# Second tile's attention in two separate parts, its moves on GpSimd's queue and its normalization on VectorE; weight loads spread over the first tile

## The chip, the cores and the metric

The kernel runs on one core of a Trainium2 chip. The core has five engines that run their own instruction streams side by side: TensorE (PE in the profile; PEld is its weight load) for matrix products, VectorE (DVE), ScalarE (ACT) and GpSimd (POOL) for elementwise work, and SyncE (SP), which here only issues DMA transfers. Other engines can issue DMAs too; each issues in the order of its own stream. The metric is the device time of one execution in microseconds (us).

## What is computed

Two stages follow each other: attention within chunks of 64 positions, and a feed-forward block with a bounded quadratic activation.

```python
scores = scale * np.matmul(q_c, k_c.transpose(0, 1, 2, 4, 3))
scores = scores - np.max(scores, axis=-1, keepdims=True)
attn = np.exp(scores)
attn = attn / (np.sum(attn, axis=-1, keepdims=True) + 1e-09)
out = np.matmul(attn, v_c)
...
h = x @ w_in
g = np.where(pos, h, np.where(neg, 0.0, (h + beta) ** 2 / (4.0 * beta)))
return (g @ w_out).astype(np.float32)
```

Here q, k and v have 8 batches, 8 heads, 576 positions of 64 numbers; x is the attention's output as 4608 tokens of 512 numbers; w_in is 512 x 2048 and w_out 2048 x 512, both given as 64-bit floats.

## The kernel before

**Tiles.** The 4608 tokens are cut into nine tiles of 512 (`t` from 0). For each tile the attention runs in four head pairs (`g` from 0 to 3), and the feed-forward in sixteen steps (`j` from 0 to 15), one for each 128 columns of w_in.

**Attention of a head pair.** `attn_turn` brings q and k into transposed form (qT, kT): for the first tile through TensorE (`flip`) and a copy by ScalarE, for later tiles by VectorE's block transposes (L372). `scores_of` and `values_of` give the two groups of 64x64 products. Between them, `attn_softmax` takes the maximum (L450), subtracts it, exponentiates and sums; the second tile instead gives the scaled negative maximum (L455) to ScalarE's exponential, which also sums (L459). Then come a small addition and a reciprocal (L476, L477), the normalization (L482: GpSimd for the first two tiles, VectorE for the others), and the transposition: for later tiles a block transpose by VectorE into the one buffer x (L504) and eight DMAs that put the blocks of x in their places in aT (`move`, L494, on SyncE's queue). Values read aT and v. `attn_split` cuts the values into a high part xh (ScalarE, L517) and a residue xl (VectorE, L518), the operands of the feed-forward. All scores and values from the second tile on share one pair of accumulation banks, ps_a.

**Feed-forward.** Products are made of three parts (high by high, high by low, low by high). `ffn_in` has twelve products for a step (L533, into ps_h), followed by ScalarE's relu and square and VectorE's bounds (r, L544); `ffn_split` makes gh and gl of r (L553, L554); `ffn_out` has twelve products for a step (L568, into four banks ps_o), two steps behind `ffn_in` (LAG). I call twelve such products a block.

**Weights.** The 32 weight pieces (wi0 to wi15, wo0 to wo15, 0.5 MB each) are loaded as 64-bit words in the first tile's time (`load_weight`) and turned into high and low 32-bit parts by `prepare`: three operations of ScalarE (L259, L265, L284) and four of VectorE (L262, L269, L274, L288). The parts take the place of the words and stay for all nine tiles. The first tile's attention borrows the places of the last weights.

**What sets the order.** The kernel's code only lists parts of work with `plan.add`: engine, an assumed cost, what is read and written. `Plan.emit` then runs a model of the engines: whenever an engine is free, it takes the part that was listed first among those that the model holds to be ready, and the instructions are emitted in this order. Each engine's stream is therefore fixed beforehand, and on the chip an instruction that has to wait holds up all that stands behind it on its engine. Where TensorE would be idle at the start, the planner puts in products without use (`warm`, L688 and L691) that keep the clock up; they end with the first use of bank ps_h1.

**Around the change.** The main loop lists, at each feed-forward step j of tile t, work of the attention of tile t+1: at j = 0, 4, 8, 12 the transposes of a head pair, at j = 2, 6, 10, 14 one part of work that has the values of a head pair and the scores of the next (`attention`, one `attn_products` call for both), with its split, its softmax and the next loads. Weight loads are listed early: twelve among the loads of the second tile's first head pairs, and up to three at each step (`load_more(3)`); they wait for nothing but their place. Two weights are prepared at each step.

## Time and profile before

| what | value |
|---|---|
| time, median of 3 runs (lowest to highest) | 885.51 us (885.17 to 887.1) |
| the profiled execution, its own time | 884.54 us |
| span of the profiled execution (first to last instruction) | 882.8 us |
| mean granted TensorE clock | 0.992 |
| ScalarE busy | 379.6 us |
| DMA, mean over the span | 72 GB/s |
| DMA, first four slices of 22 us | 213, 290, 251, 267 GB/s |

The span is 1.74 us shorter than the execution's own time. In the profile a line such as L533 is the line of the listing above. "busy" is the time in which an engine executes instructions; a row of a timeline gives start, length, engine, line, operation and tiles (written <- read), and in brackets how long the engine sat idle before it and what ended that. Lengths of neighbouring rows overlap by some hundredths of a microsecond, so a price is better taken from start to start. SPq and POOLq rows are DMA issues of these engines.

### The profile page before, as it was taken

The numbers are of one execution on the slowest core, as the hardware profiler recorded it, in microseconds if no ns is written. First come the engines' busy times: TensorE is split into PE (matmuls) and PEld (weight loads), VectorE is DVE, ScalarE is ACT, GpSimd is POOL, SyncE is SP. The second block draws the span as 40 slices with busy tenths as digits, with TensorE's granted clock in tenths as the row PEclk, the third lists the DMA queues.
The fourth block names the chain that finished last, engine by engine and source line by source line (L and its number), as shares of the span: only waits on it lengthen the run. The fifth ranks groups of instructions, "written<-read, shape, count | busy, mean of one in ns | idle before, by whom it ended". The sixth has DMA issues, their size and how long they took to land.

```text
span 882.8 us, 15026 instructions
## 1 busy us (share of the span) xinstructions
PE 863.6 (98%) x5924; PEld 707.5 (80%) x5924; DVE 451.2 (51%) x771; ACT 379.6 (43%) x691; POOL 20.2 (2%) x30
## 2 busy tenths in 40 slices
PE   9799996999999999999999999999999999999998
PEld 8688775888888888888888888888888888888886
DVE  4999994444454445444544454444444444423222
ACT  4898873333333333333433333334333333333332
POOL 6000000000000000000000000000000000000000
PEclk9999997999999999999999999999999999999999
DMA  9988335322242224222322233223222321001001
GB/s 213 290 251 267 67 67 122 54 48 49 49 96 49 48 45 100 48 49 47 92 49 47 47 72 63 47 42 79 53 48 43 66 54 25 13 1 49 0 1 48
DMA packets 265158, 63.92 MB, mean 72 GB/s; under 512 B 249984, under 2 KB 258176, under 8 KB 265088
## 3 DMA queue, kind: packets, MB, share of 16 engines
q1 hardware_dynamic: 263520, 61.65, 31.8%
q0 software_dynamic: 512, 1.05, 0.5%
q8 instruction: 47, 0.77, 0.4%
q10 hardware_dynamic: 1056, 0.26, 0.2%
q14 instruction: 23, 0.19, 0.1%
HBM read 45.09 MB, written 9.44 MB: 62 GB/s over the span
## 4 chain that ended last, share of the span: by engine, by line
PE 89%; DVE 7%; SPq 1%; issue 1%; ACT 1%; DMA 1%; POOL 0%; DVEq 0%; POOLq 0%; ACTq 0%
PE ps_h L533 42%; PE ps_o L568 41%; PE ps_a L417 2%; PE ps_a L396 2%; PE ps_h L688 1%; DVE tmp L269 1%; DVE tmp L274 1%; SPq L319 1%; DVE r L544 1%; DVE tmp L262 1%; DVE parts_wi L288 1%; SPq L494 0%; DMA q_sb<-in_q_dram 0%; DVE parts_wo L288 0%; DVE mx L450 0%
## 5 line engine op out<-in xcount | busy, mean ns | idle before, releaser
L533 PE MATMUL ps_h<-xh,parts_wi 128*128 128x512 f32 x1152 | 387.2, 396 | 4.6 <-DVE r L544 2.9
L568 PE MATMUL ps_o<-parts_wo,gh 128*128 128x512 f32 x1152 | 355.6, 390 | 1.0 <-DVE parts_wo L288 1.0
L533 PEld LDWEIGHTS ps_h<-xh,parts_wi 128*128 128x128 f32 x1152 | 218.0, 189 | 53.2 <-DVE r L544 4.0
L568 PEld LDWEIGHTS ps_o<-parts_wo,gh 128*128 128x128 f32 x1152 | 216.0, 188 | 47.0 <-DVE parts_wo L288 1.6
L544 DVE SCALAR_TENSOR_TENSOR r<-ps_h,r 128x512 f32<-128x512 f32 x144 | 98.0, 681 | 261.0 <-ACT r L543 261.0
L533 PE MATMUL ps_h<-xl,parts_wi 128*128 128x512 f32 x576 | 226.6, 393 | 1.7 <-DVE xl L518 1.7
L568 PE MATMUL ps_o<-parts_wo,gl 128*128 128x512 f32 x576 | 224.2, 389 | 0.7 <-DVE gl L554 0.7
L540 ACT ACTIVATE r<-ps_h 128x512 f32<-128x512 f32 x144 | 86.1, 598 | 284.4 <-PE ps_h L533 284.4
L553 ACT CAST gh<-r 128x512 fp32r<-128x512 f32 x144 | 89.5, 622 | 148.9 <-PE ps_o L568 114.7
L554 DVE TENSOR_TENSOR gl<-r,gh 128x512 fp32r<-128x512 f32 x144 | 98.4, 683 | 107.2 <-ACT gh L553 106.9
L533 PEld LDWEIGHTS ps_h<-xl,parts_wi 128*128 128x128 f32 x576 | 109.1, 189 | 24.7 <-DVE xl L518 3.1
L568 PEld LDWEIGHTS ps_o<-parts_wo,gl 128*128 128x128 f32 x576 | 108.1, 188 | 23.5 <-DVE gl L554 1.0
L543 ACT ACTIVATE r<-r 128x512 f32<-128x512 f32 x144 | 91.0, 632 | 3.5
L450 DVE TENSOR_REDUCE mx<-ps_a 128x8 f32<-128x512 f32 x34 | 23.4, 689 | 20.5 <-ACT xh L517 18.8
L417 PEld LDWEIGHTS ps_a<-aT,v_sb 64*64 64x64 f32 x1056 | 18.6, 134 | 15.1 <-issue 13.4
L517 ACT CAST xh<-ps_a 128x512 fp32r<-128x512 f32 x34 | 19.9, 585 | 22.0 <-PE ps_a L396 21.1
L417 PE MATMUL ps_a<-aT,v_sb 64*64 64x64 f32 x1056 | 23.2, 224 | 3.6 <-DMA aT<-x 3.6
L475 DVE TENSOR_REDUCE sm<-e 128x8 f32<-128x512 f32 x30 | 20.5, 685 | 10.1 <-ACT e L469 9.9
L504 DVE STREAM_TRANSPOSE x<-e 128x512 f32<-128x512 f32 x32 | 22.7, 710 | 2.2 <-DMA q_sb<-in_q_dram 1.2
L372 DVE STREAM_TRANSPOSE qT<-q_sb 128x512 f32<-128x512 f32 x32 | 22.5, 703 | 0.0
L518 DVE TENSOR_TENSOR xl<-ps_a,xh 128x512 fp32r<-128x512 f32 x34 | 22.3, 657 | 0.2 <-ACT xh L517 0.2
L372 DVE STREAM_TRANSPOSE kT<-k_sb 128x512 f32<-128x512 f32 x32 | 22.1, 691 | 0.0
(77 smaller groups left out, 390.1 us busy)
## 6 DMA issues: line engine op xcount, KB each, us to landing
words_wi<-in_moe_w_in_dram SPq DMA_DIRECT2D x16, 512.0 KB, 7.2
words_wo<-in_moe_w_out_dram SPq DMA_DIRECT2D x16, 512.0 KB, 7.4
v_sb<-in_v_dram SPq DMA_DIRECT2D x128, 64.0 KB, 2.4
aT<-x SPq DMA_DIRECT2D x256, 32.0 KB, 1.9
out_dram<-tmp SPq DMA_DIRECT2D x32, 256.0 KB, 2.0
q_sb<-in_q_dram SPq DMA_DIRECT2D x112, 64.0 KB, 2.3
k_sb<-in_k_dram SPq DMA_DIRECT2D x112, 64.0 KB, 2.3
q_sb<-in_q_dram SPq DMA_DIRECT2D x32, 32.0 KB, 2.1
```

The source lines that it names most:

```text
L372: plan.add("dve", 0.6, lambda src=src, dst=dst: nc.vector.transpose(out=dst, in_=src), (skey,), (dkey,))
L417: nc.tensor.matmul(out=pair[h * C:(h + 1) * C, half, HALF + n * C:HALF + (n + 1) * C], lhsT=v_sb[rows, of:of + C], rhs=aT[rows, at:at + C] ...
L450: plan.add("dve", 0.6, lambda: nc.vector.tensor_reduce(out=mx4, in_=sc, axis=AX.X, op=ALU.max), pkeys, (mkey,))
L504: plan.add("dve", 0.6, lambda: nc.vector.transpose(out=x, in_=e), (ekey,), (xkey,))
L518: plan.add("dve", 0.6, lambda: nc.vector.tensor_tensor(out=of_tokens(xl), in0=ps, in1=of_tokens(xh.bitcast(F32)), op=ALU.subtract), (*pkey ...
L533: nc.tensor.matmul(out=ps, lhsT=weight["wi", j][:, half, kc * P:(kc + 1) * P], rhs=x, start=(kc == 0 and i == 0), stop=(kc == KC - 1 and i ...
L540: plan.add("act", 0.48, lambda: nc.scalar.activation(out=r, in_=ps, func=AF.Relu, bias=0.5, scale=0.5), (pkey,), (rkey,))
L543: plan.add("act", 0.52, lambda: nc.scalar.square(out=r, in_=r), (), (rkey,))
L544: plan.add("dve", 0.6, lambda: nc.vector.scalar_tensor_tensor(out=r, in0=ps, scalar=1.0, in1=r, op0=ALU.max, op1=ALU.min), (pkey,), (rkey,))
L553: plan.add("act", 0.52, lambda: nc.scalar.copy(out=gh, in_=r), (rkey,), (ghkey,))
L554: plan.add("dve", 0.6, lambda: nc.vector.tensor_tensor(out=gl, in0=r, in1=gh.bitcast(F32), op=ALU.subtract), (rkey, ghkey), (glkey,), port ...
L568: nc.tensor.matmul(out=acc, lhsT=x[:, cols], rhs=weight["wo", j][:, half, :], start=(j == 0 and i == 0), stop=(j == NF - 1 and i == 2),)
```

## The change

Six things change.

- In the first tile's loop the second tile's attention is listed in two kinds of parts: `front` (transposes, scores, softmax) and `back` (values, split), each at a step given by the table `SECOND`. Scores and values of this tile are separate parts on TensorE. The loads of q and k follow each front, those of v each back.
- The eight moves of each head pair of the second tile are issued by GpSimd in place of SyncE.
- The normalization of the second tile runs on VectorE; GpSimd keeps the first tile's.
- Beyond the first ten, a weight load is listed with each preparation and waits for the end of that preparation (`gate`). wi0 and wi1 join the list `order`.
- The planner's assumptions differ: DMA starts at 1.4 in place of 1.68, a weight load moves for 1.4 in place of 1.7, movement is counted for each issuing engine apart, heads loaded by ScalarE or GpSimd take 1.5 times as long.
- The products without use may go on in bank ps_o1 after the first use of ps_h1, in idle time before the first output products.

```diff
-    START, START_DMA = 1.4, 1.68
+    START, START_DMA = 1.4, 1.4
...
             if moving:
-                end = moved = max(end, moved) + moving
+                end = moved[e] = max(end, moved[e]) + moving
...
-        plan.add(queue, 0.65, emit, (), (f"{w}{j}_0", f"{w}{j}_1"), lag=1.7, moving=1.7)
+        plan.add(queue, 0.65, emit, gate["ready"], (f"{w}{j}_0", f"{w}{j}_1"), lag=1.7, moving=1.4)
...
-        plan.add("dve", 0.6, low, (ykey, both[0]), (both[1],), port=True)
+        plan.add("dve", 0.6, low, (ykey, both[0]), (both[1], f"done_{w}{j}"), port=True)
+        gate["ready"] = (f"done_{w}{j}",)
...
-                (), (key,), lag=1.7, moving=rows,
+                (), (key,), lag=1.7, moving=rows if queue == "sp" else 1.5 * rows,
...
-        on_pool = t < 2
+        on_pool = t == 0
...
+        queue = "pool" if t == 1 else "sp"
...
-                    nc.sync.dma_start(
+                    queues[queue].dma_start(
...
-            plan.add("sp", 4.8, move, (xkey,), (akey,), lag=1.7, moving=0.4)
+            plan.add(queue, 4.8, move, (xkey,), (akey,), lag=1.7, moving=0.4)
...
-    load_more(4)
     load_heads(1, 0, "qk")
-    load_more(2)
+    load_next(2)
     load_heads(1, 0, "v")
-    load_more(6)
+    load_next(2)
     load_heads(1, 1)
...
+    def prepare_next():
+        if todo:
+            prepare(*todo.pop(0))
+            load_next()
...
+    def front(t, g):
+        attn_turn(t, g)
+        attn_products(scores_of(t, g))
+        attn_softmax(t, g)
+        if t == 1:
+            load_heads(*divmod(t * NP + g + 2, NP), "qk")
+
+    def back(t, g):
+        attn_products(values_of(t, g))
+        attn_split(t, g)
+        load_heads(*divmod(t * NP + g + 2, NP), "v")
+
+    SECOND = {
+        1: ((front, 0),), 3: ((front, 1),), 5: ((back, 0), (front, 2)), 8: ((back, 1), (front, 3)),
+        11: ((back, 2),), 13: ((back, 3), (front, 4)),
+    }
...
-            attention()
-            load_more(3)
+            if t == 0:
+                for what, g in SECOND.get(j, ()):
+                    what(*divmod(NP + g, NP))
+            else:
+                attention()
             if t < NTILE:
                 ffn_in(t, j)
-            for w, n in todo[:2]:
-                prepare(w, n)
-            del todo[:2]
+            prepare_next()
+            prepare_next()
...
+    def saw(writes, columns):
+        if any(k in ("ps_o0", "ps_o1") for k in writes):
+            if columns != T:
+                return columns == 0
+            fills["turns"] -= 1
+        if "ps_h1" in writes:
+            fills["bank"] = None
+        if fills["bank"] is None and not fills["turns"]:
+            fills["bank"] = o_banks[1][1]
+        return True
```

Because the planner sets the order, the diff doesn't show what stands where. In the rows below a name is the tile's own (wo15, or buffer 0 or 1 of a pair) with a running number behind it, and the changed program's lines lie some lines further down than the old one's.

The first place is TensorE's passage from the first tile to the second. Before, behind the last output products of the first tile (wo15) stood:

```order
L568 MATMUL ps_o23_111<-parts_wo15_1423,gh1_104 128x512 x2
L568 MATMUL ps_o23_111<-parts_wo15_1423,gl1_106 128x512
L417 MATMUL ps_a_112<-aT1_79,v_sb1_73 64x64 x16
L396 MATMUL ps_a_112<-kT0_75,qT0_74 64x64 x16
L533 MATMUL ps_h0_115<-xh3_1_92,parts_wi0_244 128x512
L533 MATMUL ps_h0_115<-xl3_1_100,parts_wi0_244 128x512
L533 MATMUL ps_h0_115<-xh3_1_92,parts_wi0_244 128x512
L533 MATMUL ps_h1_116<-xh3_1_92,parts_wi1_320 128x512
```

that is, the values of the second tile's last head pair (L417), the scores of the third tile's first (L396), and the products of the second tile's steps 0 and 1 that need this pair's xh3 and xl3. Now there stands:

```order
L572 MATMUL ps_o23_111<-parts_wo15_1542,gh1_104 128x512 x2
L572 MATMUL ps_o23_111<-parts_wo15_1542,gl1_106 128x512
L420 MATMUL ps_a_112<-aT0_78,v_sb0_72 64x64 x16
L399 MATMUL ps_a_112<-kT0_75,qT0_74 64x64 x16
L537 MATMUL ps_h0_115<-xh0_1_86,parts_wi2_531 128x512
L537 MATMUL ps_h0_115<-xl0_1_94,parts_wi2_531 128x512
L537 MATMUL ps_h0_115<-xh0_1_86,parts_wi2_531 128x512
L537 MATMUL ps_h0_115<-xh1_1_88,parts_wi2_531 128x512
```

These values and scores are one pair of heads later (aT0 is that of the third tile's first head pair), and only step 2 of the second tile follows: its steps 0 and 1 and the second tile's four values groups now stand ahead of this place, and the feed-forward waits for no attention here.

The second place is VectorE's work around the last two weights, wo14 and wo15. Before:

```order
L269 ISA tmp3_110<-words_wo14_721,tmp3_110 128x1024
L269 ISA tmp0_107<-words_wo15_726,tmp0_107 128x1024
L274 SCALAR_TENSOR_TENSOR tmp3_110<-words_wo14_721,tmp3_110 128x512
L274 SCALAR_TENSOR_TENSOR tmp0_107<-words_wo15_726,tmp0_107 128x512
L554 TENSOR_TENSOR gl0_105<-r0_101,gh0_103 128x512
L288 TENSOR_TENSOR parts_wo14_1417<-tmp3_110,parts_wo14_1417 128x512
L288 TENSOR_TENSOR parts_wo15_1423<-tmp0_107,parts_wo15_1423 128x512
L544 SCALAR_TENSOR_TENSOR r1_102<-ps_h1_116,r1_102 128x512
L450 TENSOR_REDUCE mx1_82<-ps_a_112 128x8
L518 TENSOR_TENSOR xl2_1_98<-ps_a_112,xh2_1_90 128x2x4x64
L455 TENSOR_SCALAR mx1_82<-mx1_82 128x8
L372 STREAM_TRANSPOSE qT0_74<-q_sb0_68 128x512
```

Now, with the sum, the normalization (L485) and the transpose (L508) of the third tile's first head pair shortly ahead of the last weights:

```order
L478 TENSOR_REDUCE sm0_83<-e0_76 128x8
L479 TENSOR_SCALAR sm0_83<-sm0_83 128x8
L480 RECIPROCAL sm0_83<-sm0_83 128x8
L290 TENSOR_TENSOR parts_wo13_1489<-tmp1_108,parts_wo13_1489 128x512
L485 TENSOR_TENSOR e0_76<-e0_76,sm0_83 128x512
L276 SCALAR_TENSOR_TENSOR tmp2_109<-words_wi15_1231,tmp2_109 128x512
L508 STREAM_TRANSPOSE x0_80<-e0_76 128x512
L548 SCALAR_TENSOR_TENSOR r0_101<-ps_h0_115,r0_101 128x512
L290 TENSOR_TENSOR parts_wi15_1505<-tmp2_109,parts_wi15_1505 128x512
```

and then

```order
L558 TENSOR_TENSOR gl0_105<-r0_101,gh0_103 128x512
L290 TENSOR_TENSOR parts_wo14_1536<-tmp3_110,parts_wo14_1536 128x512
L290 TENSOR_TENSOR parts_wo15_1542<-tmp0_107,parts_wo15_1542 128x512
L375 STREAM_TRANSPOSE qT0_74<-q_sb1_69 128x512
L548 SCALAR_TENSOR_TENSOR r1_102<-ps_h1_116,r1_102 128x512
L375 STREAM_TRANSPOSE kT0_75<-k_sb1_71 128x512
```

What moved: the maximum of the second tile's last head pair, the residues of its last two and the whole softmax of the third tile's first one stood behind the last weights, and now stand ahead of them.

The third place is ScalarE's work at the start, around the exponential of the first tile's fourth head pair (it works in the place of wo15). Before:

```order
L284 CAST parts_wo0_460<-tmp3_110 128x512
L265 ACTIVATE words_wi2_233<-words_wi2_233 128x512
L259 ACTIVATE tmp1_108<-words_wo1_240 128x512
L517 CAST xh2_0_89<-ps_a_112 128x512
L469 ACTIVATE first_wo15_118<-first_wo15_118 128x512
L265 ACTIVATE words_wo1_240<-words_wo1_240 128x512
L517 CAST xh1_0_87<-ps_o23_111 128x512
L259 ACTIVATE tmp2_109<-words_wi3_250 128x512
```

Now:

```order
L521 CAST xh0_0_85<-ps_a_112 128x512
L261 ACTIVATE tmp1_108<-words_wo1_265 128x512
L261 ACTIVATE tmp2_109<-words_wi3_271 128x512
L267 ACTIVATE words_wo1_265<-words_wo1_265 128x512
L472 ACTIVATE first_wo15_118<-first_wo15_118 128x512
L267 ACTIVATE words_wi3_271<-words_wi3_271 128x512
L521 CAST xh1_0_87<-ps_o23_111 128x512
```

The scaling of wi3's words (tmp2 <- words_wi3) stood three instructions behind this exponential and now stands two ahead of it. On GpSimd the four multiplications of the second tile are gone, and four groups of eight DMAs from x to aT stand behind those of the first tile.

More of the change, by code (lines that the diff above doesn't have):

```diff
@@ L71, in emit @@
         free["sp"] = self.START_DMA
-        port_free = moved = 0.0
+        port_free = 0.0
+        moved = dict.fromkeys(engines, 0.0)
         soon = {e: [] for e in engines}
@@ L81, in emit @@
                 offer(n)
-        fill_engine, fill_cost, fill_emit, fill_key, fill_columns = filler
+        fill_engine, fill_cost, fill_columns, fill_emit, fill_saw = filler
         filling = True
@@ L100, in emit @@
                 start, e = best
-                if filling and free[fill_engine] < start:
-                    fill_emit()
+                if filling and free[fill_engine] < start and fill_emit():
                     free[fill_engine] = self.products_end(free[fill_engine], fill_cost, fill_columns)
@@ L109, in emit @@
             _, cost, emit, _, lag, columns, port, moving, writes = parts[n]
-            filling = filling and fill_key not in writes
+            filling = filling and fill_saw(writes, columns)
             emit()
@@ L228, in turn_of @@
         return bufs[count[name] % len(bufs)]
+    gate = {"ready": ()}
     def load_weight(w, j, queue="sp"):
@@ L595, in store, with load_next @@
         plan.add("sp", 0.6, send, (okey,), (), lag=1.7, moving=0.8)
+    order = [("wi", 0), ("wi", 1)]
+    for j in range(NF):
+        order.append(("wo", j))
+        if j + 2 < NF:
+            order.append(("wi", j + 2))
+    loads = list(order)
+    def load_next(n=1):
+        for _ in range(n):
+            if loads:
+                load_weight(*loads.pop(0))
     first_loads = [
@@ L606 @@
             load_weight(which, n, queue)
+            loads.remove((which, n))
         else:
             load_heads(0, n, which, queue)
-    order = []
-    for j in range(NF):
-        order.append(("wo", j))
-        if j + 2 < NF:
-            order.append(("wi", j + 2))
     for g in range(NP):
@@ L621 @@
         attn_split(0, g)
-    loads = [o for o in order if (*o, "sp") not in first_loads]
-    def load_more(n):
-        for _ in range(n):
-            if loads:
-                load_weight(*loads.pop(0))
-    load_more(4)
     load_heads(1, 0, "qk")
-    load_more(2)
+    load_next(2)
     load_heads(1, 0, "v")
-    load_more(6)
+    load_next(2)
     load_heads(1, 1)
-    prepare("wi", 0)
-    prepare("wi", 1)
+    def prepare_next():
+        if todo:
+            prepare(*todo.pop(0))
+            load_next()
+    todo = list(order)
+    prepare_next()
[14 more added lines that the diff above has]
+    }
     LAG = 2
-    todo = list(order)
     for t in range(NTILE + 1):
@@ L642 @@
             n = (t + 1) * NP + j // 4
-            if (t, j) == (0, 0):
-                attn_turn(1, 0)
-                attn_products(scores_of(1, 0))
-                attn_softmax(1, 0)
             def attention():
@@ L655, in attention @@
                     if n + 1 < ALL:
-                        attn_products(
-                            values_of(*now), scores_of(*then), lag=0.0 if t == 0 else 0.8
-                        )
+                        attn_products(values_of(*now), scores_of(*then), lag=0.8)
                         attn_split(*now)
@@ L665, in attention @@
                         load_heads(*divmod(n + 2, NP))
-            attention()
-            load_more(3)
+            if t == 0:
[3 more added lines that the diff above has]
+                attention()
             if t < NTILE:
                 ffn_in(t, j)
-            for w, n in todo[:2]:
-                prepare(w, n)
-            del todo[:2]
+            prepare_next()
+            prepare_next()
             m = t * NF + j - LAG
@@ L680 @@
     nc.vector.memset(zeros.bitcast(F32), 0.0)
-    fills = {"n": 0}
+    fills = {"n": 0, "turns": 2 * NP, "bank": h_banks[1][1]}
     def warm():
@@ L685, in warm @@
         fills["n"] += 1
-        ps = h_banks[1][1]
+        ps = fills["bank"]
+        if ps is None:
+            return False
         if n < 28 or n >= 52:
             nc.tensor.matmul(out=ps[:, :P], lhsT=ident, rhs=ident, start=True, stop=True)
-            return
-        cols = (256, 384, T)[(n - 28) // 8]
-        nc.tensor.matmul(
-            out=ps[:, :cols], lhsT=zeros[:, :P], rhs=zeros[:, :cols], start=True, stop=True
-        )
-    plan.emit(("pe", 0.215, warm, "ps_h1", 512))
+        else:
+            cols = (256, 384, T)[(n - 28) // 8]
+            nc.tensor.matmul(
+                out=ps[:, :cols], lhsT=zeros[:, :P], rhs=zeros[:, :cols], start=True, stop=True
+            )
+        return True
[8 more added lines that the diff above has]
+            fills["bank"] = o_banks[1][1]
+        return True
+    plan.emit(("pe", 0.215, 512, warm, saw))
 _INS = ['q', 'k', 'v', 'moe_w_in', 'moe_w_out']
```

## The prediction

> **What bounds the kernel now.** I read the page first, then the windows by stage, then the chain of waits around the end of the first tile, then VectorE's timeline.
>
> ```profile
> span 882.8 us, 15026 instructions
> PE 863.6 (98%) x5924; PEld 707.5 (80%) x5924; DVE 451.2 (51%) x771; ACT 379.6 (43%) x691; POOL 20.2 (2%) x30
> ...
> DVE  4999994444454445444544454444444444423222
> ```
>
> TensorE (PE) is busy for 98% of the span, so only the rest and any time at a lower clock can be won. VectorE (DVE) averages 51%, but its slices say where: 9 from the second to the sixth slice (22 us each), 4 to 5 after.
>
> The windows give each stage's busy time per engine, with instruction counts, and TensorE's granted clock behind them:
>
> ```profile
> 97.00:131.00 34.00, 32.27 (x252) 24.49 (x251) 33.87 (x63) 27.61 (x79) 2.48 (x2) 1.00 0.36 64
> 131.00:149.00 18.00, 11.29 (x100) 8.12 (x98) 8.10 (x16) 5.76 (x15) 1.04 (x1) 0.83 0.59 135
> ...
> 300.00:400.00 100.00, 100.00 (x675) 82.21 (x675) 46.20 (x77) 37.45 (x63) 0.00 (x0) 1.00 0.30 58
> ```
>
> At 97 to 131 us VectorE is full (33.87 of 34.00) and TensorE starts to wait. At 131 to 149 us both idle, and the clock falls to 0.83. From 300 to 400 us TensorE never idles. The loss lies before 154 us. The chain of waits (start, length, what) names it:
>
> ```profile
> 134.62 0.64 SPq L494
> ...
> 139.24 1.93 DMA aT<-x
> ...
> 141.30 0.63 PE ps_a L417 x27
> ...
> 146.36 0.70 DVE sm L475
> 147.08 0.18 DVE sm L476
> ...
> 148.87 4.95 PE ps_h L533 x12
> 153.82 2.74 PE ps_o L568 x12
> 156.56 0.68 PE ps_h L533 x3
> 157.24 0.62 PE ps_a L417 x32
> 157.87 0.47 PE ps_a L396 x32
> 158.33 2.27 PE ps_h L533 x9
> 160.60 2.72 PE ps_o L568 x12
> ```
>
> The last head pair of the second tile is late: SyncE issues its eight moves from 134.62, they land at 141.17, and only then do its values products run (141.30). The next twelve products take 4.95 us where twelve take 2.72 at full clock (160.60). I take as **marker** the start of the second tile's first output block, 153.82; behind it TensorE is full in both programs, so the change is worth what it moves this point. After the marker the old program still does one values-and-scores pair (157.24 to 158.33, 1.09 us; the split block takes 0.68 + 2.27 = 2.95 for 2.72, so 1.32 in all), which the new order does before it. So saving = 153.82 + 1.32 - M, with M the new marker.
>
> **The change part by part.** *The pair's wait goes.* In the new order all four values blocks of the second tile lie inside the first tile's feed-forward. What is late next is VectorE, which must prepare all weights and do the attention before the first tile can end. So M follows from when VectorE has prepared the last two weights, wo14 and wo15. VectorE's timeline of before:
>
> ```profile
> 33.53 1.26 DVE L274 SCALAR_TENSOR_TENSOR tmp<-words_wi,tmp 128x512 uint32<-128x512 uint32 x1
> ...
> 50.38 1.53 DVE L288 TENSOR_TENSOR parts_wi<-tmp,parts_wi 128x512 fp32r<-128x512 f32 x1
> ...
> 99.45 1.58 DVE L262 TENSOR_SCALAR tmp<-tmp 128x512 uint32<-128x512 uint32 x2
> ...
> 114.30 0.75 DVE L262 TENSOR_SCALAR tmp<-tmp 128x512 uint32<-128x512 uint32 x2
> ...
> 115.97 0.69 DVE L288 TENSOR_TENSOR parts_wi<-tmp,parts_wi 128x512 fp32r<-128x512 f32 x1
> 116.58 0.69 DVE L544 SCALAR_TENSOR_TENSOR r<-ps_h,r 128x512 f32<-128x512 f32 x1
> 117.18 0.94 DVE L274 SCALAR_TENSOR_TENSOR tmp<-words_wo,tmp 128x512 uint32<-128x512 uint32 x1
> 118.04 0.70 DVE L504 STREAM_TRANSPOSE x<-e 128x512 f32<-128x512 f32 x1
> 118.67 0.65 DVE L269 CUSTOM_DVE_ANT_0 tmp<-words_wi,tmp 128x1024 uint16<-128x1024 uint16 x1
> ...
> 125.92 1.29 DVE L288 TENSOR_TENSOR parts_wo<-tmp,parts_wo 128x512 fp32r<-128x512 f32 x2
> ```
>
> No idle time stands in these rows. By starts, an operation on 128x512 costs 0.60 (115.97 to 116.58), a transpose 0.62. The last row is wo14 and wo15: wo14 is ready at 126.5. Counted in the two orders, VectorE does these more ahead of that row: two residues xl (1.2), two maxima (1.2), one scaling of a maximum (0.16), one subtraction (0.6), one sum (0.7, row 146.36), two pairs of small operations (0.8, from 0.18 each and the gaps), two x transposes (1.24), two more q and k transposes (1.24), and **five normalizations** (3.0), four of them taken from GpSimd: 10.1 us. Against it, a GpSimd multiplication held VectorE up: 1.53 for 0.69 (50.38), 1.58 for 0.75 (99.45), 0.94 for 0.69 (117.18), 1.9 us in all, which go. So the four normalizations that change engine cost nearly nothing net; what costs is attention that used to come behind the weights. Net +8.2: wo14 at 134.7.
>
> *The start.* VectorE's first 37 operations are the same set; in the old program the next begins at 33.53, of which 0.6 is a GpSimd multiplication's hold (1.26 for 0.69). In the new order ScalarE must scale the words of wi3 before the exponential of the fourth pair:
>
> ```profile
> 22.70 0.43 SPq L237 DMA_DIRECT2D words_wi<-in_moe_w_in_dram  x1
> ...
> words_wi<-in_moe_w_in_dram SPq DMA_DIRECT2D x1, 512.0 KB, 6.9
> ...
> 30.88 0.62 ACT L469 ACTIVATE first_wo<-first_wo 128x512 f32<-128x512 f32 x1
> ```
>
> wi3 lands at 22.70 + 6.9 = 29.6; two ScalarE operations later (about 1.1) the exponential starts at 30.7, as before (30.88). But behind it VectorE now has eight of the 37 left (sum, two small, two xl, a shift, a residue, an addition: 3.8), so it passes this point at about 35.2, 1.65 late, less what of the 0.6 hold falls into this wait. I take 1.5; bounds 0 (same operations) and 2.6 (with a wait for xh in it).
>
> *Small waits* of VectorE for exponentials, now closer behind their maxima: 0 to 2, I take 0.8. wo14 is then ready at 137.0.
>
> *From there to the marker* TensorE does four blocks (2.72 each: out 14, in 1 of the next tile, out 15, in 2) and the pair (1.32): M = 137.0 + 0.1 + 10.9 + 1.3 = 149.3. Saving 155.14 - 149.3 = **5.8 us**. The dive of the clock goes with the wait.
>
> *Moves on GpSimd.* Four times eight issues leave SyncE and go to GpSimd; nothing else stands behind them there after the first tile. The rows are of GpSimd's timeline, then VectorE's beside its issues, then the DMA issues (KB, us to landing):
>
> ```profile
> 1.44 5.03 POOL L338 DMA_DIRECT2D v_sb<-in_v_dram  x8
> ...
> 10.38 1.25 POOL L338 DMA_DIRECT2D first_wo<-in_v_dram  x2 [0.20 <-issue]
> ...
> 50.08 1.29 POOL L482 TENSOR_TENSOR e<-e,sm 128x512 f32<-128x512 f32 x1 [15.83 <-DVE sm L477]
> ```
>
> ```profile
> 11.43 0.68 DVE L269 CUSTOM_DVE_ANT_0 tmp<-words_wi,tmp 128x1024 uint16<-128x1024 uint16 x1
> 12.03 0.68 DVE L466 TENSOR_TENSOR e<-ps_a,mx 128x512 f32<-128x512 f32 x1
> ```
>
> ```profile
> words_wo<-in_moe_w_out_dram SPq DMA_DIRECT2D x16, 512.0 KB, 7.4
> aT<-x SPq DMA_DIRECT2D x256, 32.0 KB, 1.9
> ...
> v_sb<-in_v_dram POOLq DMA_DIRECT2D x8, 64.0 KB, 6.0
> first_wo<-in_v_dram POOLq DMA_DIRECT2D x8, 64.0 KB, 7.1
> ```
>
> Eight issues take 5.0 (1.44); a landing costs between 1.9 (same move from SyncE) and 7.1 (GpSimd's loads, beside a burst), so a move takes 7 to 12 us. The tightest user is the first values block: the order puts twelve VectorE operations (7.2) and two blocks (5.4) between the transpose and it, 12.7 us. The next x transpose, which also waits for the move, is 13.9 us away, later ones over 16. Hidden, by 0.6 at worst; uncovered, each us would cost at most one.
>
> *Weight loads* each wait for a preparation. They run ten weights ahead, some 21 us of VectorE work (0.34 and three times 0.60 for each weight); a landing is 7.4: hidden. In SyncE's queue the loads of heads stand behind a waiting one. *Planner constants, fillers* in a free bank: priced inside the start.
>
> **Rivals.** *GpSimd's issues hold VectorE*, as its multiplications do (50.38). If each of 32 issues held it for its 0.62, wo14 would be 20 us later: 885.5 - 5.8 + 20 = about 899.5, slower; it decides from 0.18 per issue. Against it: beside the issues at 10.38 VectorE keeps 0.60 from start to start (11.43 to 12.03). These are few rows.
>
> *The moves starve.* GpSimd's issues might wait for VectorE's operations. If each of eight waited for one double-rate operation (a shift, 0.75 for two at 114.30, so 0.38), a move would take 5.0 + 3.0 + 7.1 = 15.1, 2.4 more than the 12.7 to the first values block: about 882.1. For more than that no row speaks. The Trainium skill (SBUF — State Buffer, "A bandwidth-pool intuition that's wrong (but worth ruling out)") says that a GpSimd-issued DMA of about 620 ns takes about 3100 ns beside a VectorE copy, because descriptors can't be written while VectorE holds the shared port. By it eight issues would be an estimated 24.8 us, VectorE would wait at three x transposes some 30 us in all, and the time would be near 910; no row here has the two together at full load.
>
> *The new order's waits eat the gain*: a gated load that comes late costs up to its landing, 7.4, which gives 885.5 - 5.8 + 7.4 = 887; half of it 883.4. For it: VectorE had no idle time to lose before, so any wait is new; against it the lead of ten weights.
>
> *The start is no later and nothing waits*: saving 8.1 or more, 877.4.
>
> **How the numbers follow.** The profiled execution took 884.54 (span 882.8 and 1.74 around it), the median is 885.51; the forecast is 885.51 - 5.8 = **879.7** (878.7 on the profiled one's scale). With the bounds of the start and the small waits it is 877.4 to 882.0. Chances: as worked out 0.63; waits of the new order 0.17 (882 to 887); GpSimd's issues hold VectorE 0.12 (over 888); the moves starve by the page's price 0.03; better than 877.4 0.05. The range 876.5 to 886.5 keeps about 0.82. A measurement tells some 0.2%, 1.8 us, from no change: faster 0.63 + 0.05 + 0.08 = 0.76, same 0.06, slower 0.12 + 0.03 + 0.03 = 0.18.
>
> **What would show it.** Right: no stretch of TensorE idle between 131 and 149 us and clock 1.00 there; VectorE without gaps until its last weight residue, near 137 us; marker near 149; values blocks that don't wait for aT. Wrong: VectorE's operations lengthened beside GpSimd's issues; a transpose x or values block released by aT's landing; scaling that waits for words; or a marker near 149 with an unchanged end, which would mean that later tiles are not full.

## The result, and the profile after

The changed kernel takes 881.61 us (median of 4 runs, 880.04 to 881.89); the kernel before takes 885.34 beside it (4 runs, 884.62 to 887.1). The ratio is 0.9948, with a 95% interval of 0.9936 to 0.996: faster by 0.5%, where 0.65% (5.8 us) was forecast. The profiled execution took 881.89.

The page's first lines for the changed kernel (span, busy time by engine, VectorE's 40 slices), then the windows of the same stages as before:

```profile
span 879.8 us, 15029 instructions
...
PE 862.1 (98%) x5914; PEld 705.9 (80%) x5914; DVE 454.7 (52%) x775; ACT 378.6 (43%) x691; POOL 34.1 (4%) x58
...
DVE  3999897444444445444544454444444444423222
```

```profile
97.00:131.00 34.00, 32.14 (x184) 25.32 (x184) 31.77 (x59) 26.43 (x48) 4.96 (x8) 0.91 0.43 108
131.00:149.00 18.00, 17.55 (x131) 13.98 (x135) 13.23 (x23) 8.46 (x15) 0.00 (x0) 1.00 0.31 60
300.00:400.00 100.00, 100.00 (x675) 82.22 (x675) 45.99 (x77) 37.03 (x62) 0.00 (x0) 1.00 0.30 57
```

The old hole is closed: from 131 to 149 us TensorE is busy for 17.55 (11.29 before) at clock 1.00 (0.83). But 97 to 131 us now has a mean clock of 0.91, and 46.8 to 97 us has new idle time (before, then after):

```profile
46.80:97.00 50.20, 50.20 (x281) 41.45 (x280) 50.05 (x92) 44.04 (x96) 1.29 (x1) 1.00 0.78 223
```

```profile
46.80:97.00 50.20, 46.56 (x368) 35.38 (x366) 49.94 (x97) 44.26 (x116) 14.07 (x24) 0.99 0.96 255
```

So some 6 us of TensorE's time and a clock of 0.83 were won at the end of the first tile, and 3.6 us of idle time and a clock of 0.91 for 34 us were paid ahead of it. The chain of waits behind 130 us, with the marker (first output block of the second tile) at 152.22:

```profile
134.05 2.57 PE ps_h L537 x10
136.62 0.68 PE ps_o L572 x3
137.30 2.72 PE ps_h L537 x12
140.02 2.72 PE ps_o L572 x12
142.74 2.72 PE ps_h L537 x12
145.46 2.72 PE ps_o L572 x12
148.18 0.62 PE ps_a L420 x32
148.80 0.47 PE ps_a L399 x32
149.27 2.95 PE ps_h L537 x12
152.22 2.72 PE ps_o L572 x12
```

TensorE's last waits ahead of this chain are for wo13 and wi15:

```profile
131.05 0.50 PE L572 MATMUL ps_o<-parts_wo,gh 128*128 128x512 f32 x1 [1.00 <-DVE parts_wo L290]
...
134.05 0.73 PE L537 MATMUL ps_h<-xh,parts_wi 128*128 128x512 f32 x2 [0.40 <-DVE parts_wi L290]
```

155.14 - 152.22 = 2.9 us saved by the prediction's count, and the span is 3.0 shorter: later tiles are as full as before, and all of the difference lies ahead of the marker. VectorE's rows at both ends of its busy stretch, and its one large gap:

```profile
35.30 0.70 DVE L375 STREAM_TRANSPOSE qT<-q_sb 128x512 f32<-128x512 f32 x1
...
106.08 0.69 DVE L290 TENSOR_TENSOR parts_wi<-tmp,parts_wi 128x512 fp32r<-128x512 f32 x1 [2.16 <-ACT parts_wi L286]
...
137.60 1.29 DVE L290 TENSOR_TENSOR parts_wo<-tmp,parts_wo 128x512 fp32r<-128x512 f32 x2
```

The first row is the one behind VectorE's first 37 operations, the last is wo14 and wo15. Where the gap comes from shows in TensorE's timeline, the granted clock by windows of 2.5 us, and ScalarE's timeline:

```profile
95.36 0.90 PE L420 MATMUL ps_a<-aT,v_sb 64*64 64x64 f32 x32 [1.73 <-ACT e L462]
...
97.57 0.79 PE L572 MATMUL ps_o<-parts_wo,gh 128*128 128x512 f32 x1 [0.76 <-DVE parts_wo L290]
```

```profile
97.50:100.00 2.50, 2.43 (x6) 1.95 (x7) 2.50 (x6) 2.50 (x6) 0.92 (x2) 0.50 0.49 87
100.00:102.50 2.50, 2.50 (x8) 1.92 (x7) 2.50 (x5) 1.14 (x3) 2.50 (x5) 0.50 0.81 150
```

```profile
104.39 0.60 ACT L544 ACTIVATE r<-ps_h 128x512 f32<-128x512 f32 x1 [3.25 <-PE ps_h L537]
```

TensorE waits twice, its clock falls to 0.50, the block from 100.07 takes 4.30 us in place of 2.72, ScalarE's relu of that block waits for it and holds the cast of the next weight behind it, and VectorE, the engine whose work sets the end, sits idle for 2.16 us. This is the chain that the first experiment tests.

### The profile page after: what moved, and what is told of

Read it like the earlier page. It is cut to its first block, busy times and chain, and to the rows that moved or that the text cites. A ratio compares the mean times of both kernels' runs of the same rounds, so it can differ in the third digit from the quotient of the medians.

```text
span 879.8 us, 15029 instructions
## 1 busy us (share of the span) xinstructions
PE 862.1 (98%) x5914; PEld 705.9 (80%) x5914; DVE 454.7 (52%) x775; ACT 378.6 (43%) x691; POOL 34.1 (4%) x58
## 4 chain that ended last, share of the span: by engine, by line
PE 86%; DVE 7%; SPq 3%; DMA 1%; issue 1%; ACT 1%; DVEq 0%; ACTq 0%
PE ps_h L537 42%; PE ps_o L572 41%; PE ps_a L420 2%; SPq L308 2%; PE ps_a L399 2%; DVE tmp L271 1%; DVE tmp L276 1%; DMA words_wi<-in_moe_w_in_dram 1%; DMA q_sb<-in_q_dram 1%; DVE parts_wo L290 1%; DVE r L548 1%; SPq L239 1%; DVE gl L558 1%; DVE tmp L264 0%; DVE parts_wi L290 0%
## 5 line engine op out<-in xcount | busy, mean ns | idle before, releaser
L557 ACT CAST gh<-r 128x512 fp32r<-128x512 f32 x144 | 89.8, 624 | 151.7 <-PE ps_o L572 114.1
L508 DVE STREAM_TRANSPOSE x<-e 128x512 f32<-128x512 f32 x32 | 22.7, 711 | 0.9
```

Source lines behind the costliest of these rows:

```text
L508: plan.add("dve", 0.6, lambda: nc.vector.transpose(out=x, in_=e), (ekey,), (xkey,))
L557: plan.add("act", 0.52, lambda: nc.scalar.copy(out=gh, in_=r), (rkey,), (ghkey,))
```

## The experiments

Each kernel was timed beside the kernel before; ratios are to that one (the change: 0.9948). Three VectorE and TensorE moments of the profiled execution are compared: the first row above (start), the last weight pair, and the marker (with the prediction's 1.32 us added where the pair of values and scores stands behind it). The kernels of this table have the same instructions of VectorE and ScalarE up to the start, so marker minus start leaves out how the way there went:

| kernel | ratio (95%) | start | last pair | marker | marker - start |
|---|---|---|---|---|---|
| the change | 0.9948 (0.9936 to 0.996) | 35.30 | 137.60 | 152.22 | 116.9 |
| values group later | 0.9965 (0.9953 to 0.9977) | 34.97 | 135.90 | 152.08 | 117.1 |
| third tile later | 0.9917 (0.9905 to 0.9928) | 34.13 | 131.61 | 148.18 | 114.1 |
| moves on SyncE | 1.0016 (1.0008 to 1.0025) | 34.27 | 141.91 | 156.53 | 122.3 |
| normalization on GpSimd | 0.9958 (0.9946 to 0.997) | 35.05 | 135.29, 136.65 | 151.75 | 116.7 |
| loads not gated | 0.9954 (0.9936 to 0.9972) | 35.86 | 136.98 | 151.60 | 115.7 |
| third tile later, normalization on GpSimd | 0.9907 (0.9889 to 0.9925) | 32.94 | 128.60 | 145.64 | 112.7 |
| wait filled | 0.9932 (0.9918 to 0.9947) | 34.07 | 133.95 | 149.48 | 115.4 |

The start itself lies between 32.94 and 35.86 in these eight executions: a part of the scatter between runs. Each kernel was profiled once, and the column of differences scatters too: the kernel with loads not gated, whose time can't be told from the change's, lies 1.2 us below it there. Differences of that size show little.

**Values group later.** The third head pair's values group is moved away from the scores that it waited behind: the planner is told that the fourth pair's exponentials (`g == 3`) come 2 us later, and so lists other products ahead of it.

```diff
-            plan.add("act", 2.33, exps, (*pkeys, mkey), (ekey, skey))
+            plan.add("act", 2.33, exps, (*pkeys, mkey), (ekey, skey), lag=2.0 if g == 3 else 0.0)
```

> The values products of the second tile's third head pair stand some three blocks of products later on TensorE (they stood one block behind the fourth pair's scores, in the same accumulation banks). My theory: in the changed kernel they waited 1.73 us for the fourth pair's exponentials, the clock fell to 0.5, a block took 4.30 in place of 2.72, and ScalarE, held behind that block, left VectorE idle for 2.16 us; that is 2 of the 3 us that the marker came late. Without it: marker 152.2 - 2.2 = about 150.0, time 881.6 - 2.2 = about 879.4, and no VectorE idle over 1 us between 90 and 110 us. Rival, VectorE's load alone sets the end and the waits only turn up elsewhere: marker 151.9 to 152.5, time 881.3 to 881.9. Second rival, TensorE is bound at its end by the weights wi15 and then runs without a gap, whatever comes before: marker within 0.3 of 152.2 although the idle at 106 is gone.

881.49 us, marker 152.08: my theory failed in its price. TensorE's waits in this kernel:

```profile
95.50 0.50 PE L572 MATMUL ps_o<-parts_wo,gh 128*128 128x512 f32 x1 [2.24 <-ACT parts_wo L286]
...
130.56 0.80 PE L572 MATMUL ps_o<-parts_wo,gl 128*128 128x512 f32 x1 [2.30 <-DVE gl L558]
```

Without the values group in its way TensorE waits just as long in the same place, for wo8. The shared bank was the last to release it, not the cause; the preparation of the weights is late there. The clock falls again, VectorE's gap is gone and the last pair comes 1.4 us earlier from the start. That is given back at 130.56, where TensorE waits for a residue that stands behind the third tile's softmax in VectorE's stream (the clock falls to 0.50 once more, and a block takes 3.76 us). The first rival is right, its waits turn up elsewhere: what VectorE does near the last weights sets the end, and its order there is tested next. The second rival's marker fits as well, but TensorE doesn't run without a gap, and what it waits for is gl, not wi15.

**Third tile later.** So this work is moved behind the last weights.

```diff
-        11: ((back, 2),), 13: ((back, 3), (front, 4)),
+        11: ((back, 2),), 13: ((back, 3),), 15: ((front, 4),),
```

> The third tile's first head pair (transposes, scores, softmax) is listed two steps later, so that its VectorE work stands behind the last weights: two q and k transposes 1.24, maximum 0.6, subtraction 0.6, sum 0.7, small operations 0.4, normalization 0.6, one transpose 0.6, in all 4.7 us. My theory (VectorE's work ahead of the last weights sets the end): wo14 ready 4 to 5 us earlier, at 133 to 134, and the time 878 to 879.5, since TensorE's own work takes over as the bound before all 4.7 are gained. Rival, TensorE's waits and clock between 95 and 105 us set it: wo14 earlier, but the time 881.6 within 0.5. Second rival, the postponed head pair is late for its own values and TensorE waits behind the marker: over 882.5.

877.73 us, 0.8% below the kernel before. The last pair comes 4.8 us earlier from the start (131.61 - 34.13 = 97.5, against 102.3), as the 4.7 us of postponed work say, and TensorE doesn't wait any more behind 97 us; of the 4.8, 2.9 reach the marker. The waits and the low clock at 92 to 102 us are unchanged in it (0.50, 0.50 and 0.67 from 95 to 102.5 us).

**Moves on SyncE.**

```diff
-        queue = "pool" if t == 1 else "sp"
+        queue = "sp"
```

> The four times eight moves go back to SyncE's queue, all else as in the changed kernel. My theory: their queue matters little, since neither a transpose into x nor a values block waited for them, and VectorE was held by some 0.1 us in each group of eight: 881.6 within 0.6, VectorE's last residue within 0.5 us of 137.6. Rival, GpSimd's issues hold VectorE noticeably: faster by over 1 us. Second rival, moves that wait in SyncE's queue hold up the gated weight loads behind them, which is what the other queue was good for: slower by over 1 us, with ScalarE's scaling waiting for words.

886.12 us: my expectation failed by 4.5 us, more than the whole gain. SyncE's queue around the first move, and VectorE and TensorE at its landing:

```profile
48.42 4.72 SPq L322 DMA_DIRECT2D q_sb<-in_q_dram  x4
53.24 2.60 SPq L322 DMA_DIRECT2D k_sb<-in_k_dram  x4
...
56.49 5.68 SPq L498 DMA_DIRECT2D aT<-x  x8
```

```profile
63.69 0.71 DVE L508 STREAM_TRANSPOSE x<-e 128x512 f32<-128x512 f32 x1 [3.99 <-DMA aT<-x]
```

```profile
61.07 0.30 PE L420 MATMUL ps_a<-aT,v_sb 64*64 64x64 f32 x2 [2.09 <-DMA aT<-x]
63.61 1.12 PE L420 MATMUL ps_a<-aT,v_sb 64*64 64x64 f32 x30 [2.24 <-DMA aT<-x]
```

The block x is written at 45.23 and its move is issued at 56.49, behind loads of q and k whose eight issues take 7.3 us. It is the second rival's kind of mishap with the roles changed: not moves that hold up loads, but loads that hold up moves. In the kernel before the distance is longer (x at 51.84, its move at 75.73, behind loads of q, k and v and fourteen weights) but does no harm, since the first values group comes at 92.41 only. So the other queue is what lets this order work, though a landing from it took longer beside the weight loads. The rows are DMA issues (KB each, median us from issue to landing): GpSimd's in the changed kernel, SyncE's in this one from 55 to 95 us, and GpSimd's last eight in the kernel with the split undone (below), from 115 to 130 us, when no weights were being loaded:

```profile
aT<-x POOLq DMA_DIRECT2D x32, 32.0 KB, 5.2
```

```profile
aT<-x SPq DMA_DIRECT2D x24, 32.0 KB, 2.2
```

```profile
aT<-x POOLq DMA_DIRECT2D x8, 32.0 KB, 1.9
```

Those last eight land as fast as SyncE's moves do (1.9 for the 256 of the kernel before): GpSimd's queue alone doesn't make a landing slow.

**Normalization on GpSimd.**

```diff
-        on_pool = t == 0
+        on_pool = t < 2
```

> The second tile's normalization goes back to GpSimd, all else as in the changed kernel. By the terms of the prediction it takes 2.4 us of VectorE's own work away (4 x 0.6) and brings back its holds (1.9 us for four multiplications by before's rows): VectorE's last residue 0.5 us earlier or later, time 881.6 within 0.8. Rival, the two engines' shared stretch costs far more than the rows say: slower by over 2 us. Second rival, it costs nothing and VectorE gains the 2.4: 879.2.

880.11 us, marker minus start 0.2 us less than in the change: as the prediction priced it, the engine of these four multiplications makes no difference that can be told. VectorE has no gap here and comes to wo14 2.1 us earlier from the start (135.29 - 35.05 = 100.2), about the gap's 2.16, so four multiplications less make its own stretch no shorter; TensorE then waits 1.88 us for gl at 129.95, as in the first experiment.

**Split undone.** Values of one head pair and scores of the next are one part again.

```diff
-                        attn_products(values_of(*now), scores_of(*then), lag=0.8)
+                        attn_products(values_of(*now), scores_of(*then), lag=0.0 if t == 0 else 0.8)
...
-            if t == 0:
-                for what, g in SECOND.get(j, ()):
-                    what(*divmod(NP + g, NP))
-            else:
-                attention()
+            if (t, j) == (0, 0):
+                attn_turn(1, 0)
+                attn_products(scores_of(1, 0))
+                attn_softmax(1, 0)
+            attention()
```

> The changed kernel with the first tile's loop as before: values of one head pair and scores of the next are one part again, at steps 2, 6, 10 and 14; GpSimd's queue, VectorE's normalization, gated loads and the planner's numbers stay as changed. In this program's order VectorE has nearly the same work ahead of the last weights as in the changed one (117.9 against 119.1 us by the prediction's prices), and the fourth values group stands ahead of the first tile's end here too. Theory now (the weights' preparation on VectorE sets the end, and the moves' queue lets the attention come early): within 1.5 us of the changed kernel, 880 to 883. Rival, the separate parts are what brings the gain: 884.5 or more, with a wait of TensorE for the second tile's attention over 1 us in the first tile's second half.

885.39 us, ratio 0.9992 (0.9973 to 1.0012). The ten times fall into two groups, four from 880.9 to 881.5 and six from 885.4 to 887.5; the profile is one of the second. So the rival's time is right for six of ten executions, where the gain is gone; in the other four it is that of the change. TensorE in the profile, and its clock from 55 to 60 us:

```profile
55.68 1.02 PE L420 MATMUL ps_a<-aT,v_sb 64*64 64x64 f32 x27 [2.93 <-DMA aT<-x]
...
77.05 0.63 PE L420 MATMUL ps_a<-aT,v_sb 64*64 64x64 f32 x27 [2.15 <-DMA aT<-x]
```

```profile
55.00:60.00 5.00, 4.32 (x68) 3.75 (x69) 1.80 (x5) 1.10 (x2) 0.00 (x0) 0.50 0.81 137
```

A joined part puts the values early, beside the scores, and they wait for the move's landing (GpSimd issues from 45.44 for 4.65, then the landing). Behind the wait the clock falls to 0.50. Apart, as in the change, the first values group runs at 59.94 and waits for nothing. The four shorter executions have a mean granted clock of 0.997 to 0.998, the six others 0.992 to 0.994, so the shorter ones lost less of the clock; none of them was profiled. The old hole is closed in this kernel too: from 131 to 149 us TensorE is busy for 17.30 us at clock 1.00. What is lost is lost in the first half of the tile's time, not in the second, where the rival had put it.

**Split alone**, in the kernel before, with `front`, `back` and the table `SECOND` as in the change (their lines are left out here).

```diff
-            attention()
+            if t == 0:
+                for what, g in SECOND.get(j, ()):
+                    what(*divmod(NP + g, NP))
+            else:
+                attention()
```

> The kernel before with the separate parts and their table alone; moves on SyncE, the normalization on GpSimd, loads listed early, planner's numbers as before. Theory: the moves again stand behind loads of heads in SyncE's queue, so that a transpose into x or values products wait for aT some 2 to 4 us, and the gain is lost: 884 to 887. Rival, the separate parts alone bring it: 880.5 to 882.5.

879.99 us, ratio 0.9943 (0.9922 to 0.9965): the rival is right. The separate parts alone bring all that the whole change brings. The first move still leaves SyncE only at 74.90, but with the attention so late TensorE stays full until 100 us (50.20 of 50.20 at 46.8 to 97); what is lost lies at two waits behind that, with the clock at 0.52 and 0.56 behind them:

```profile
104.32 0.69 PE L396 MATMUL ps_a<-kT,qT 64*64 64x64 f32 x32 [2.51 <-DVE xl L518]
...
114.61 0.69 PE L417 MATMUL ps_a<-aT,v_sb 64*64 64x64 f32 x30 [2.09 <-DMA aT<-x]
```

**Loads not gated.**

```diff
-        gate["ready"] = (f"done_{w}{j}",)
```

> The changed kernel with weight loads that wait for nothing but their place; they are listed as in the changed one. By the prediction the gate costs and brings nothing: 881.6 within 0.8, no scaling that waits for words in either. Rival, without the gate the weights' loads crowd out the loads of q, k and v, and the second tile's attention starts later: over 883, with VectorE or TensorE waiting for q_sb or k_sb between 26 and 60 us.

880.7 us, inside the interval of the change: the gate neither brings nor costs anything that can be told, as predicted.

**Third tile later and normalization on GpSimd** (the two edits above together).

> The third tile's first head pair two steps later (877.7 by itself) and the second tile's normalization on GpSimd (880.1 by itself), together. Theory, VectorE's work sets the end until TensorE runs without a gap: since TensorE waits no more behind 97 us with the first edit alone, the second can only help ahead of that point, 0 to 1.5 us: 876.2 to 877.7. Rival, both edits shorten the same queue and add up: 876.2 or less (877.7 - 1.5). Second rival, GpSimd's multiplications hold VectorE more than they spare it once there is no idle time: 878 or more.

876.63 us (875.04 to 877.53), the lowest median of the study, inside the theory's range and near its end toward the rival. Its profile has no fall of the clock at all (mean 1.00), though TensorE waits there as elsewhere; see the last section.

**Planner's numbers back.**

```diff
-    START, START_DMA = 1.4, 1.4
+    START, START_DMA = 1.4, 1.68
...
-                end = moved[e] = max(end, moved[e]) + moving
+                end = moved = max(end, moved) + moving
...
-        plan.add(queue, 0.65, emit, gate["ready"], (f"{w}{j}_0", f"{w}{j}_1"), lag=1.7, moving=1.4)
+        plan.add(queue, 0.65, emit, gate["ready"], (f"{w}{j}_0", f"{w}{j}_1"), lag=1.7, moving=1.7)
...
-                (), (key,), lag=1.7, moving=rows if queue == "sp" else 1.5 * rows,
+                (), (key,), lag=1.7, moving=rows,
```

> The changed kernel with the planner's numbers of before (start of DMAs 1.68, a weight's movement 1.7, one count of movement for all engines); parts, queue, normalization and gate as changed. ScalarE then has the fourth pair's exponential ahead of the scaling of wi3 again. Theory, the planner's numbers cost the start (the prediction's 1.5 us): VectorE's first 37 operations end 1 to 1.7 us earlier than at 35.3, no VectorE idle over 0.5 us before 32 us, and the marker and the time follow: 880.0 to 880.7. Rival, the start is made up by later waits: 881.6 within 0.5. Second rival, the order that these numbers give the rest of the first tile is worse: over 882.

880.0 us, ratio 0.9945 (0.9928 to 0.9962). By time this can't be told from the change. In the profile VectorE's idle time at 31 us is gone and the first q transpose starts at 33.91 with one operation (0.6) more ahead of it, so the start is some 1.3 us earlier than the mean of the eight in the table (34.57), but not earlier than the earliest of them (32.94). The wait is there in all nine kernels with the change's numbers (0.35 to 1.48 us) and in none of the five with those of before, so its cause is shown; what it is worth in the end is not.

**Wait filled.** Twelve products without use, whose result nothing reads, keep TensorE busy around the values group.

```diff
...
+            useless(8)
             for n in range(CT // 2):
...
+            useless(4)
```

> The changed kernel with twelve products without use (8 ahead of the third head pair's values group, 4 behind it, about 2.6 us) in a bank that is free there, so that TensorE is busy through its wait at 93 to 97 us; no other instruction moves. Theory, idle time brings the clock down: granted clock 1.00 from 95 to 105 us (0.79, 0.50, 0.50, 0.85 in the changed kernel), the block behind it in 2.72 in place of 4.30, VectorE's idle time of 2.16 us at 106 gone, last weights 1.5 to 2.2 us earlier. If the clock's loss is on the path the marker comes 1.5 to 2.2 earlier (150 to 150.7, time 879.4 to 880.1); if VectorE's order near the last weights sets the end, as the first experiment says, TensorE waits some 2 us for gl near 130 instead and the marker stays within 0.5 of 152.2. Rival, the clock falls for another reason than idleness: clock and marker as in the changed kernel.

878.79 us. Granted clock in the same windows:

```profile
95.00:97.50 2.50, 2.50 (x19) 2.02 (x15) 2.50 (x6) 2.50 (x6) 0.00 (x0) 1.00 0.72 125
97.50:100.00 2.50, 2.50 (x13) 2.07 (x12) 2.50 (x6) 2.40 (x5) 2.13 (x4) 1.00 0.65 117
100.00:102.50 2.50, 2.50 (x13) 2.07 (x12) 2.50 (x6) 1.94 (x4) 2.50 (x5) 1.00 0.83 263
```

As the theory has it: with TensorE busy the clock stays at 1.00, VectorE has no gap, and the last pair comes 2.4 us earlier from the start (99.9 against 102.3). One profile could show this by chance (see the last section), but the mean clock of all six executions is 0.997 to 1.00, against 0.993 to 0.998 for the change's four. 1.5 of the 2.4 reach the marker, little more than the 1.2 by which the kernel with loads not gated differed; the rest goes at a new wait near the end, of 1.23 us at 127.42 for wo13, after which the clock falls again (0.68 and 0.64). Between the two prices that I had given (2 us or nothing) it lies nearer the first. The intervals of the two ratios overlap, so by time the gain is not certain.

**Split alone, third tile later.** The edit of the second experiment in the kernel of the sixth.

> The kernel before with the separate parts alone (880.0), and in them the third tile's first head pair two steps later (worth 3.9 us in the changed kernel). Theory, in the program with the separate parts alone TensorE runs without a gap from 117 us on, so what VectorE does near the last weights is already off the path: the same within 1 us, 879 to 881, and what is left is the wait at 102 to 115 us with its clock. Rival, the postponed work pays here as there: 876 to 877.5.

879.63 us, ratio 0.9942 (0.9929 to 0.9954): no change against 879.99. Where TensorE runs without a gap behind 117 us, postponed work on VectorE is worth nothing, as the theory said.

**Combined.** Planner's numbers of before, third tile later, normalization on GpSimd, and eight products without use ahead of the values group.

> The changed kernel with what helped in the runs so far: the planner's numbers of before (880.0 by itself), the third tile's first head pair two steps later and the second tile's normalization on GpSimd (876.6 together), and eight products without use ahead of the third head pair's values group (twelve around it gave 878.8 by itself). Theory: each shortens another piece of the path, start, last weights and the clock between 95 and 105 us, so most of it adds: 876.6 - 1.6 for the start - 0 to 1 for the clock = 874 to 875.5, TensorE without a wait over 1 us behind 97 us. Rival, they shorten the same piece and TensorE's own work is the bound: 876 to 877.5. Second rival, the eight products stand in a place without a wait in this order and cost their 1.7 us: 877 or more, with VectorE full around them and the marker no earlier.

876.97 us, ratio 0.9913 (0.99 to 0.9927), from 876.82 to 877.25 only. The first rival is right: TensorE is full from 26.7 us on, at clock 1.00.

```profile
46.80:97.00 50.20, 50.14 (x407) 40.86 (x406) 49.33 (x91) 44.82 (x118) 18.84 (x28) 1.00 1.04 255
97.00:131.00 34.00, 33.88 (x174) 26.57 (x173) 33.17 (x61) 27.43 (x50) 4.62 (x8) 1.00 0.35 98
```

But some of it is work without use: the added products take 1.79 us at 94.35 on the chain of waits. It beats both kernels, and its times lie closer together than those of any other; it is not below the 876.63 without fillers.

## Why the prediction was right, and where it was off

The time, 881.61, lies in the range and on the forecast side; the saving is 2.9 of 5.8 us by the profiled executions (3.7 by the medians). By its own steps:

- *The pair's wait goes*: shown. No wait of it is left, and the clock is 1.00 from 131 to 149 us. The separate parts alone are enough for the gain (879.99). They are not the only thing that closes the hole: with the parts joined and the moves on GpSimd it is closed too, but two waits for landings at 55.68 and 77.05 then come in its place, and in six of ten executions they take the gain.
- *VectorE's added work*, +8.2: from the start to the last pair it takes 102.3 us, before 92.4 (33.53 to 125.92); of the 9.9 more, 2.16 are the gap, so the work is 7.7. Right within 0.5.
- *The start*, 1.5: 1.8 in this execution (35.30 against 33.53), 1.0 for the mean of eight. Right in kind; the place scatters by 2.9 us over the eight executions of the table, which I didn't know.
- *Small waits*, 0.8 within 0 to 2: 2.16, just outside. This term was mis-sized: it counted VectorE's waits for exponentials, and the wait that came is one for TensorE, through a fall of the clock and ScalarE's queue. The prediction had a clock in the old hole only.
- *From there to the marker*, 12.3: 14.0. **The step that failed is "M follows from when VectorE has prepared the last two weights, wo14 and wo15".** TensorE was not waiting for wo14 (ready at 138.2, used at 140.02): it had waited for wo13 and wi15 at 131 and 134 us and was still busy with the blocks behind these. The third tile's softmax stands ahead of those weights in VectorE's stream, and moving it away was worth 2.9 us. TensorE's waits of 1.00 and 0.40 us for the two and one of 0.34 ahead of them are together 1.74 us, all that this term lacks; the 2.9 is more, since the last weights themselves come earlier then. The blocks and the pair themselves take 12.2 us (140.02 to 152.22), as priced.
- These add up: start +0.3, work -0.5, waits +1.4, and the last step +1.7 make 2.9, the distance of the marker from its forecast (152.22 - 149.3).
- *Moves on GpSimd*, hidden: right for this queue. The rival that issues hold VectorE is out: beside eight issues its operations start 0.60 apart.

```profile
47.62 4.64 POOL L498 DMA_DIRECT2D aT<-x  x8 [14.33 <-issue]
```

```profile
48.69 0.68 DVE L558 TENSOR_TENSOR gl<-r,gh 128x512 fp32r<-128x512 f32 x1
49.29 0.68 DVE L276 SCALAR_TENSOR_TENSOR tmp<-words_wo,tmp 128x512 uint32<-128x512 uint32 x1
```

- So is *the moves starve*: eight issues take 4.6 to 5.0 us beside a full VectorE, and no transpose or values group waits for aT. The Trainium skill's 3100 ns for such an issue (SBUF — State Buffer, "A bandwidth-pool intuition that's wrong (but worth ruling out)") is not seen here; an issue takes about 0.6 us. What the prediction lacked is the other side: with the new order the old queue would have cost 4.5 us.
- *Normalization* and *weight loads*: no difference that can be told, as priced.

## What to carry to other kernels

When a wait at the end of a stage is taken away, look for the bound in everything that feeds the stage's last steps, not in its last operand: here the work that had been ordered ahead of the last four weights cost 2.9 us and could stand behind them. A new wait of an engine with a clock of its own can cost more than its length, since the work behind it may run slower and the engines that feed on it idle. A transfer that stands between two dependent steps should not share a queue with loads that may wait; here a free queue was worth 4.5 us, although the landings took longer on it.

## What was not expected of the hardware

Waits of 1.2 to 2.9 us (the shortest is the 1.23 of the filled kernel, with one of 0.34 ahead of it) were followed by a fall of TensorE's clock to 0.50, and the same waits need not bring it. TensorE's waits at the third values group, first in the kernel with the normalization on GpSimd, then in the one that has the third tile later as well:

```profile
94.87 0.90 PE L420 MATMUL ps_a<-aT,v_sb 64*64 64x64 f32 x32 [1.49 <-ACT e L462]
...
97.10 0.79 PE L572 MATMUL ps_o<-parts_wo,gh 128*128 128x512 f32 x1 [0.90 <-DVE parts_wo L290]
```

```profile
92.74 0.90 PE L420 MATMUL ps_a<-aT,v_sb 64*64 64x64 f32 x32 [1.48 <-ACT e L462]
...
94.97 0.50 PE L572 MATMUL ps_o<-parts_wo,gh 128*128 128x512 f32 x1 [0.90 <-DVE parts_wo L290]
```

The same two waits, 1.49 and 0.90 us or 1.48 and 0.90 us, lead to 0.50 in one (from 97.05 to 100.46) and leave 1.00 in the other. The clock records of the traces show what they differ in. In each of the fourteen traces the moments at which the clock changes lie whole multiples of 3.41 us apart; in the first kernel these are 97.05, 100.46, 131.18 and 134.60. I divided both traces into stretches of 3.41 us at these moments; in the second kernel a border lies at 92.66, 24 stretches behind its change at 10.74. The stretches with the waits, the first kernel's, then the second's:

```profile
93.64:97.05 3.41, 1.33 (x33) 0.95 (x33) 3.38 (x8) 3.41 (x13) 1.04 (x1) 1.00 0.93 219
```

```profile
89.25:92.66 3.41, 2.01 (x9) 1.31 (x7) 3.41 (x8) 2.97 (x18) 0.00 (x0) 1.00 0.95 246
92.66:96.08 3.42, 2.44 (x38) 1.88 (x39) 3.38 (x8) 3.42 (x8) 1.04 (x1) 1.00 0.87 214
```

In the first both waits fall into one stretch, in which TensorE idles for 2.08 us; in the second the border parts them, into 1.40 and 0.98. Counted over all fourteen traces, from 20 us to the last 8, the clock fell behind 20 such stretches, each with 1.54 to 3.12 us idle, and behind none with less; five with 1.55 to 1.68 idle brought no fall, so in that narrow band either happens. What decides is how much of the idle time lies between two borders, and the borders lie elsewhere in each trace (11.09 in the changed kernel, 11.72 and 10.74 in these two): by this the same waits can cost much or nothing by chance. No experiment moved a border, so the rule rests on these counts. The Trainium skill (TensorE: Matmul & The Clock Gate, "HAM oscillation — how this bites in real kernels") asks that there be no idle gaps over about 3.4 us; here the clock fell after single gaps of half that length. The same page ("What's actually happening") says that activity is watched in windows that run freely; the borders found here agree with it.
